# A threshold that two engines may take, and two accumulators in one tile

## The chip, the cores and the metric

The kernel runs on one core of one Trainium2 chip. The metric is the device time of one execution in microseconds (us). The engines are named as in the profile: PE (TensorE matmul), PEld (its weight loads), DVE (VectorE), ACT (ScalarE), POOL (GpSimd) and SP (the queue that issues most transfers).

## The reference

Eight batches, eight heads, 576 positions, head size 64. Attention keeps only the scores that lie within tau of their row's maximum; the result, seen as x of 512 channels, goes through a gated mixing layer:

```python
scores = scale * np.matmul(q, k.transpose(0, 1, 3, 2))
thresh = np.max(scores, axis=-1, keepdims=True) - tau
scores = np.where(scores >= thresh, scores, -1000000000.0)
attn = np.exp(scores - np.max(scores, axis=-1, keepdims=True))
attn = attn / (np.sum(attn, axis=-1, keepdims=True) + 1e-09)
attn_out = np.matmul(attn, v)
x = attn_out.transpose(0, 2, 1, 3).reshape(B, S, H * D)
gate_pre = sum(conv_w[k] * xp[:, k:k + S, :] for k in range(5))   # xp: x shifted in by 4 zeros
gate = 1.0 / (1.0 + np.exp(-gate_pre))
out = (gate * (x @ w_val)) @ w_out
```

## The kernel before, in words

**Tiles.** The work is cut into 32 jobs, one for each pair of heads of a batch. A job has nine score tiles of 128 rows by 576 keys: four for each head and one that holds the last 64 rows of both heads. There are 288 such tiles in all. For each tile PE makes the scores `s` in one of two PSUM rooms (`multiply`, L498), DVE finds the negated row maximum into column 0 of `nm` (`largest`, L502), and ACT makes the exponential `e` (`weigh`, L508). The threshold is one number for each row: the maximum less tau. It goes into column 1 of `nm`, and in the kernel before ACT computes it right behind the exponential (L510), as part of the same planned operation. DVE then masks the exponential where the score reaches the threshold, and sums the row (`keep`, L524); this frees the room of `s`. POOL adds a small constant to the sums (L541), DVE takes the reciprocal (L543), POOL or ACT divides (L554, L550), PE transposes (L604) into two `tp` rooms, and ACT copies the transposed tile to `T` (L615).

**Halves and accumulators.** When the tiles of half a job are there, PE multiplies `T` by `v` into an accumulator `acc` (`attend`, L643 and L650), and ACT copies it to `xT` (L658). A half is 320 or 256 columns. After the fourth job of a batch come the products with `w_val` and `w_out` (`products`, L742): 16 groups of 12 matmuls for each batch, each group into an accumulator. A group's result leaves through DVE (`g`, L769, for `w_val`) or ACT (`o`, L807, for `w_out`). So there are 64 accumulations of each of the three kinds. Each matmul of a product must follow the one before it. There are two accumulator rooms, `r_acc`, shared by all three kinds; in the kernel before they are two tiles of their own, [P, 512] each, one PSUM bank each.

**Order.** Nothing is issued in the order of the code. `op` describes an operation: the engine or engines that may do it, a due time, a cost and a time after which its result is there, what it must follow, which rooms it takes and which it gives back. `carry_out` then picks, again and again, the operation that can begin first (the earlier due time wins among equals), emits it on its engine, and so writes the instruction stream of every engine. An operation with more than one way (`other=`) goes to the engine where it can begin first. Before, only the division has two ways, POOL and ACT (`DIVIDE`). Each engine executes its own stream in that order. The waits between engines come from a layer below, which looks at which tiles an instruction reads and writes and adds semaphore waits.

Of the kernel before, what the change touches and what calls it, by code (L numbers as in the profile page):

```python
# [10 lines left out]
F32 = mybir.dt.float32  # L11
# [3 lines left out]
AF = mybir.ActivationFunctionType  # L15
# [2 lines left out]

P = 128
AHEAD = False  # L20
TH = "ACT"
DIVIDE = ("ACT",)
DUE = (8, 8, 8)
PACE_M = 0.17


@with_exitstack
def tile_thresholded_attention_gated_mix(
# [149 lines left out]
    r_s = Rooms(ps_s, 2, [P, 2, 512], F32, "s")  # L178
# [63 lines left out]
    class Words:  # L242


        def __init__(self, u, name, w, c, d0, before):
            due = u * 3.0 - 4
# [33 lines left out]
    def subtract(due, n, get, after, takes=(), gives=()):  # L280


        w = n // 2
        for cols in (slice(0, w), slice(w, n)):
            def run(cols=cols):
                dst, whole, high = get()
                nc.gpsimd.tensor_sub(dst[:, cols], whole[:, cols], high[:, cols].bitcast(F32))  # L287

            cost = w * 0.00237 + 0.04
            after = [op("POOL", due, cost, cost + 0.1, run, after, takes)]  # L290
            takes = ()
        after[0].gives = list(gives)
        return after[0]


    class Job:


        def __init__(self, i, b, g, at):
            self.i, self.b, self.g, self.at = i, b, g, at  # L300
            due = at - 9

            def fetch_v():
                self.v = r_v.take()
                nc.sync.dma_start(self.v, vs[b, g])

            self.got_v = op("SP", at - 3, 0.5, 3.6, fetch_v, takes=[r_v])
            if i == 0:
                self.load_at_once()
            else:  # L310
                self.prepare(due)

        def prepare(self, due):
# [24 lines left out]
            def low_q():  # L338
                if not hasattr(self, "ql"):
                    self.ql = r_ql.take()  # L340
                return self.ql, self.q_r, self.qh

            def scale_q():
                nc.gpsimd.tensor_scalar(self.q_r, self.q_r, sc, 0.0, op0=ALU.mult, op1=ALU.add)

# [4 lines left out]
            scaled = op("POOL", due, 0.75, 0.86, scale_q, [got_q])  # L350
            high = op("ACT", due + 1, 0.58, 0.76, high_q, [scaled], [r_qh])
            low = subtract(due + 2, S, low_q, [high], [r_ql], [(r_qr, lambda: self.q_r)])

            def place(which):
                def run():
# [91 lines left out]
    class Tile:  # L447
        def __init__(self, k, t, h, qc, grp):
            self.k, self.t, self.h, self.qc, self.grp = k, t, h, qc, grp
            i = h or 0  # L450
            both = h is None
            if both:
                after = [t.high_k, t.low_k, *t.blocks]
            elif t.i == 0:
                after = [t.first[h]]
            else:
                after = t.copied
            if tiles:
# [25 lines left out]

        def multiply(self):
            t, h, qc = self.t, self.h, self.qc
            s = self.s = r_s.take()
            for a in range(2):
                hs = slice(a * HS, (a + 1) * HS)
                if h is None:  # L490
# [15 lines left out]
        def weigh(self):  # L506
            self.e = r_e.take()
            nc.scalar.activation(self.e, self.s[:, :, :HS], AF.Exp, bias=self.nm[:, 0:1])  # L508
            if TH == "ACT":
                nc.scalar.activation(  # L510
                    self.nm[:, 1:2], self.nm[:, 0:1], AF.Identity, bias=less, scale=-1.0
                )

        def level(self):
            nc.vector.tensor_scalar(
# [14 lines left out]
    class Group:  # L530
# [5 lines left out]
        def turned(self, k):  # L536
# [4 lines left out]
            add = op("POOL", k - 4, 0.2, 0.33, lambda: nc.gpsimd.tensor_scalar(  # L541
                sums(), sums(), 1.0, 1e-9, op0=ALU.mult, op1=ALU.add), [self.kept])
            inv = op("DVE", k - 4.9, 0.08, 0.33, lambda: nc.vector.reciprocal(ri(0, n), sums()), [add])  # L543
            divided = []

            def divide(i, engine):
# [11 lines left out]
            others = {"DVEp": (0.44, 0.57), "ACT": (0.68, 0.83)}  # L558
            for i in range(n):
                divided.append(op(  # L560
                    "POOL", k - 4 + 0.1 * i, 0.74, 0.82, divide(i, "POOL"), [inv],
                    gives=[(r_sums, lambda: self.sums)] if i == n - 1 else [],
                    other=[(e, *others[e], divide(i, e)) for e in DIVIDE],
                ))
            if self.both:
                divided.append(op("POOL", k - 4, 0.21, 0.3, lambda: spread(
                    self.p[:, S : S + SL], self.p[:, S - SL : S]), divided))
            parts = [(0, NKC), (NKC, 1)] if self.both else [(0, 3), (3, 3), (6, 3)]
            out = []
            for c0, m in parts:  # L570
                last = c0 + m == (NKC + 1 if self.both else 2 * NKC + 1)
                half = self.half
                turn = op(
                    "PE", k - 3 + 0.1 * c0, 0.109 * m, 0.109 * (m - 1) + 0.35, self.turn(c0, m),
                    divided if last else divided[0 : 1 + c0 // 3 * (n - 1)], [r_tp],
                    [(r_pl if self.both else r_pp, lambda: self.p)] if last else [],
                )
# [2 lines left out]
                if not half.begun:  # L580
                    takes, half.begun = [r_T], True
                out.append(op(
                    "ACT", k - 3 + 0.1 * c0, cost, cost + 0.17, self.copy(c0, m), [turn, *half.room], takes,
                    [(r_tp, lambda c0=c0: self.tp[c0])],
                ))
                if takes:
# [44 lines left out]
    class Half:  # L631
# [4 lines left out]
        def attended(self, k):  # L636
# [18 lines left out]
            def evacuate():  # L655
                if j == 0:
                    t.xT = r_xT.take()
                nc.scalar.copy(t.xT[:, x0 : x0 + w], self.acc[:, :w])  # L658
# [5 lines left out]
            made = op("PE", k - 2, cost, cost + 0.2, attend, [t.got_v, *self.copies], [r_acc], gives)  # L664
            cost = 0.31 if j == 0 else 0.255
            after = [made] if j == 0 else [made, t.got_x]
            t.got_x = op("ACT", k - 4, cost, cost + 0.2, evacuate, after, [r_xT] if j == 0 else [],
                         [(r_acc, lambda: self.acc)])


    class Batch:
# [182 lines left out]
    for t in jobs:  # L854
# [3 lines left out]
        for j in range(2):  # L858
# [12 lines left out]
        convolve(t, batch, len(tiles))  # L871
        if t.g == NP - 1:
            last = products(batch, len(tiles) + 4.0, last)
    carry_out()


# [41 lines left out]
```

## Time and profile before

| | |
|---|---|
| time, median of 3 runs | 766.35 us (765.61 to 766.81) |
| the profiled execution | 766.39 us, its span 764.6 us |
| PE busy | 714.2 us (93%), 5216 matmul records |
| DVE busy | 617.5 us (81%) |
| ACT busy | 640.9 us (84%) |
| POOL busy | 544.1 us (71%) |
| granted TensorE clock, mean | 0.990 |
| chain that ended last | PE 71%, DVE 8%, ACT 7%, POOL 6%, DMA 4%, issue 3% |

A group of instructions is shown as line, engine, operation, output and inputs, shapes and count, then busy us and mean ns of one, then the idle time before them and what ended it. Matmuls are pipelined: the distance of two starts is what one costs the engine, and a record's own length is longer than that, with an end that is modelled.

### The profile page before, as it was taken

The numbers are of one execution on the slowest core, as the hardware profiler recorded it, in microseconds if no ns is written. First come the engines' busy times: TensorE is split into PE (matmuls) and PEld (weight loads), VectorE is DVE, ScalarE is ACT, GpSimd is POOL, SyncE is SP. The second block draws the span as 40 slices with busy tenths as digits, with TensorE's granted clock in tenths as the row PEclk, the third lists the DMA queues.
The fourth block names the chain that finished last, engine by engine and source line by source line (L and its number), as shares of the span: only waits on it lengthen the run. The fifth ranks groups of instructions, "written<-read, shape, count | busy, mean of one in ns | idle before, by whom it ended". The sixth has DMA issues, their size and how long they took to land.

```text
span 764.6 us, 15851 instructions
## 1 busy us (share of the span) xinstructions
PE 714.2 (93%) x5216; PEld 602.7 (79%) x5216; DVE 617.5 (81%) x1308; ACT 640.9 (84%) x1469; POOL 544.1 (71%) x885
## 2 busy tenths in 40 slices
PE   3687889979999999999999999999999999999997
PEld 3465557767788888888888888888888888888897
DVE  5878999989888878888888787888778988888630
ACT  5788987888889989989998898899889898988832
POOL 3677777778778867787678776688668876775431
PEclk9989999999999999999999999999999999999999
DMA  6746635344665556555555456455455455540001
GB/s 186 182 127 162 168 106 121 109 116 122 177 169 135 129 145 155 154 120 127 141 141 130 124 141 171 123 130 151 123 141 135 125 147 156 141 107 20 32 32 63
DMA packets 51890, 99.05 MB, mean 130 GB/s; under 512 B 9056, under 2 KB 9056, under 8 KB 51808
## 3 DMA queue, kind: packets, MB, share of 16 engines
q1 hardware_dynamic: 51488, 97.47, 49.0%
q8 instruction: 42, 0.69, 0.4%
q10 hardware_dynamic: 320, 0.56, 0.3%
q14 instruction: 40, 0.33, 0.1%
HBM read 35.74 MB, written 9.44 MB: 59 GB/s over the span
## 4 chain that ended last, share of the span: by engine, by line
PE 71%; DVE 8%; ACT 7%; POOL 6%; DMA 4%; issue 3%; SPq 1%; POOLq 0%; ACTq 0%
PE acc L742 20%; PE s L498 17%; PE acc L650 15%; PE tp L604 14%; PE acc L643 4%; DVE nm L502 3%; DMA q_r<-qT 2%; DVE pp L524 2%; ACT e L508 2%; ACT T L615 1%; DVE pre L700 1%; POOL pp L554 1%; POOL xl L287 1%; DMA KL<-kl 1%; POOL gl L287 1%
## 5 line engine op out<-in xcount | busy, mean ns | idle before, releaser
L502 DVE TENSOR_REDUCE nm<-s 128x1 f32<-128x576 f32 x288 | 215.8, 753 | 54.0 <-PE s L498 50.4
L508 ACT ACTIVATE e<-s,nm 128x576 f32<-128x576 f32 x288 | 215.5, 748 | 25.1 <-DVE nm L502 13.0
L524 DVE SCALAR_TENSOR_TENSOR pp<-s,nm,e 128x576 f32<-128x576 f32 x256 | 207.3, 813 | 35.1 <-ACT nm L510 31.7
L615 ACT COPY T<-tp 128x384 f32<-128x384 f32 x384 | 175.3, 487 | 27.6 <-PE tp L604 26.0
L604 PE MATMUL tp<-ident,pp 128*128 128x128 f32 x1152 | 182.3, 277 | 13.0 <-POOL pp L554 6.6
L498 PE MATMUL s<-KH,Q 128*128 128x288 f32 x512 | 162.1, 332 | 19.2 <-DVE Q L434 8.8
L554 POOL TENSOR_SCALAR pp<-pp,sums 128x576 f32<-128x576 f32 x174 | 142.5, 824 | 36.5 <-DVE sums L543 25.2
L604 PEld LDWEIGHTS tp<-ident,pp 128*128 128x128 f32 x1152 | 139.3, 142 | 23.2 <-POOL pp L554 10.1
L498 PE MATMUL s<-KL,Q 128*128 128x288 f32 x512 | 145.9, 299 | 0.7 <-DMA KL<-kl 0.7
L650 PE MATMUL acc<-T,v 128*64 128x256 f32 (+1 forms) x1024 | 138.3, 412 | 0.0
L498 PEld LDWEIGHTS s<-KH,Q 128*128 128x128 f32 x512 | 99.2, 194 | 43.3 <-DVE pp L524 13.8
L700 DVE SCALAR_TENSOR_TENSOR pre<-xT,cw,pre 128x576 f32<-128x576 f32 x128 | 119.2, 931 | 11.1 <-POOL pre L693 11.0
L650 PEld LDWEIGHTS acc<-T,v 128*64 128x64 f32 x1024 | 67.8, 136 | 62.9 <-issue 24.9
L498 PEld LDWEIGHTS s<-KL,Q 128*128 128x128 f32 x512 | 99.1, 194 | 0.9 <-DMA KL<-kl 0.9
L510 ACT ACTIVATE nm<-nm,less 128x1 f32<-128x1 f32 x288 | 85.0, 295 | 0.0
L742 PE MATMUL acc<-gl,woh 128*128 128x320 f32 (+1 forms) x256 | 78.1, 305 | 4.1 <-POOL gl L287 4.1
L742 PE MATMUL acc<-xl,wvh 128*128 128x320 f32 (+1 forms) x256 | 78.7, 307 | 2.6 <-POOL xl L287 2.5
L541 POOL TENSOR_SCALAR sums<-sums 128x2 f32<-128x2 f32 (+1 forms) x160 | 47.5, 297 | 45.5 <-DVE pp L524 33.2
L742 PE MATMUL acc<-gh,woh 128*128 128x320 f32 (+1 forms) x256 | 78.9, 308 | 0.7 <-ACT o L807 0.7
L742 PE MATMUL acc<-xh,wvl 128*128 128x320 f32 (+1 forms) x256 | 79.3, 310 | 0.0
L742 PE MATMUL acc<-xh,wvh 128*128 128x320 f32 (+1 forms) x256 | 78.4, 306 | 0.7 <-DVE g L769 0.5
L742 PE MATMUL acc<-gh,wol 128*128 128x320 f32 (+1 forms) x256 | 78.4, 306 | 0.0
(79 smaller groups left out, 1273.9 us busy)
## 6 DMA issues: line engine op xcount, KB each, us to landing
KH<-kh SPq DMA_DIRECT2D x124, 144.0 KB, 2.5
KL<-kl SPq DMA_DIRECT2D x124, 144.0 KB, 3.2
k_r<-kT SPq DMA_DIRECT2D x32, 320.0 KB, 3.7
v<-vs SPq DMA_DIRECT2D x32, 320.0 KB, 3.0
q_r<-qT SPq DMA_DIRECT2D x32, 288.0 KB, 2.9
outT<-o SPq DMA_DIRECT2D x32, 288.0 KB, 2.2
Q<-qh SPq DMA_DIRECT2D x62, 128.0 KB, 2.3
Q<-ql SPq DMA_DIRECT2D x62, 128.0 KB, 2.5
```

Source lines behind the costliest of these rows:

```text
L498: nc.tensor.matmul(s[:, a, :HS], w, m, start=i == 0, stop=i == len(terms) - 1)
L502: nc.vector.tensor_reduce(self.nm[:, 0:1], self.s[:, :, :HS], axis=AX.XY, op=ALU.max, negate=True)
L508: nc.scalar.activation(self.e, self.s[:, :, :HS], AF.Exp, bias=self.nm[:, 0:1])
L510: nc.scalar.activation(self.nm[:, 1:2], self.nm[:, 0:1], AF.Identity, bias=less, scale=-1.0)
L524: nc.vector.scalar_tensor_tensor(grp.p[:, i * S : (i + 1) * S].rearrange("p (a f) -> p a f", a=2), self.s[:, :, :HS], self.nm[:, 1:2], self.e,
L541: add = op("POOL", k - 4, 0.2, 0.33, lambda: nc.gpsimd.tensor_scalar(sums(), sums(), 1.0, 1e-9, op0=ALU.mult, op1=ALU.add), [self.kept])
L554: nc.gpsimd.tensor_scalar(v, v, ri(i), 0.0, op0=ALU.mult, op1=ALU.add)
L604: nc.tensor.transpose(tp[:, i * P : (i + 1) * P], self.p[:, k0 : k0 + P], ident)
L615: nc.scalar.copy(T[:, c0 : c0 + n, self.off : self.off + P], tp[:, 0 : n * P].rearrange("p (c q) -> p c q", q=P),)
L650: nc.tensor.matmul(acc[hs, :w], t.v[:, c0 : c0 + D], T[:, h * NKC + c, :], start=False, stop=c == NKC - 1, skip_group_check=True,)
L700: nc.vector.scalar_tensor_tensor(cv, t.xT[:, i : i + S], cw[:, g, i : i + 1], cv, op0=ALU.mult, op1=ALU.add)
L742: nc.tensor.matmul(taken[name, e, j][:, :w], wt[:, c, c0 : c0 + P], moving(c, i)[:, hs], start=n == 0, stop=n == NM - 1,)
```

## The change

The constant `TH` names two engines now, and the threshold becomes a planned operation of its own, apart from the exponential. It has two ways: on DVE (`level`) or on ACT (`level_act`), with a due time a little ahead of the exponential's. The exponential's planned cost falls from 0.83 to 0.64. Both must be there before `keep`.

The same diff turns several numbers of the planner into named constants of the same value (`AHEAD_D`, `AHEAD_T`, `AHEAD_A`, `AHEAD_J`, `LATE_X`, `LATE_M`, `CONVERT`), adds ways that are switched off (`SUB`, `QS`, `EXTRA`), and takes the two accumulators from one tile [P, 2, 512], of which each room is a half `accs[:, i, :]`.

```diff
-TH = "ACT"
+TH = ("DVE", "ACT")
 DIVIDE = ("ACT",)
+SUB = False
+EXTRA = 0
+QS = False
...
+    class Scores(Rooms):
+
+
+        def __init__(self, *args):
+            super().__init__(*args)
+            self.extra = None
+
+        def give(self, room, when):
+            if self.extra is not None and room is self.extra and retired:
+                self.extra = None
+                for i in range(2):
+                    r_acc.give(room[:, i, :], when)
+            else:
+                super().give(room, when)
+
+    retired = []
+    r_s = Scores(ps_s, 2, [P, 2, 512], F32, "s")
     r_tp = Rooms(ps_t, 2, [P, 512], F32, "tp")
-    r_acc = Rooms(ps_a, 2, [P, 512], F32, "acc")
+    r_acc = Rooms(ps_a, 1, [P, 2, 512], F32, "acc")
+    if EXTRA:
+        r_s.extra = r_acc.take()
+        r_s.give(r_s.extra, 0.0)
+    else:
+        accs = r_acc.take()
+        for i in range(2):
+            r_acc.give(accs[:, i, :], 0.0)
...
             if TH == "ACT":
                 after = [op("ACT", k - DUE[1], 0.83, 1.0, self.weigh, [largest], [r_e])]
             else:
+                ways = {"ACT": (0.19, 0.33, self.level_act), "DVE": (0.13, 0.2, self.level)}
+                first, *rest = TH
                 after = [
                     op("ACT", k - DUE[1], 0.64, 0.78, self.weigh, [largest], [r_e]),
-                    op("DVE", k - 9, 0.13, 0.13, self.level, [largest]),
+                    op(first, k - 8.5, *ways[first], [largest], other=[(w, *ways[w]) for w in rest]),
                 ]
...
+        def level_act(self):
+            nc.scalar.activation(
+                self.nm[:, 1:2], self.nm[:, 0:1], AF.Identity, bias=less, scale=-1.0
+            )
+
         def level(self):
             nc.vector.tensor_scalar(
                 self.nm[:, 1:2], self.nm[:, 0:1], -1.0, less, op0=ALU.mult, op1=ALU.add
...
             def attend():
-                acc = self.acc = r_acc.take()
+                acc = self.acc = rooms.take()
...
+            rooms = r_tp if EXTRA and t.b == 0 and k < EXTRA + 4 else r_acc
```

The planner's new choices give every engine another order of the same work. By the built streams, 124 of the 288 thresholds stand on DVE and 164 on ACT; 161 of those 164 stand directly ahead of an exponential. ACT has 106 divisions instead of 86, POOL 182 instead of 202. All other operations keep their engines and counts. Three places show what the prediction speaks of. In brackets is the engine whose semaphore an instruction waits for.

DVE at the first tiles of the run, before (TENSOR_REDUCE makes the maximum, the SCALAR_TENSOR_TENSOR on `pp` is the masking) and then now:

```order
L502 TENSOR_REDUCE nm_125<-s_101 128x1 [waits PE_49]
L502 TENSOR_REDUCE nm_126<-s_102 128x1 [waits PE_49]
L224 TENSOR_SCALAR cw_173<-cw_raw 128x20 [waits DMAHW0_49]
L524 SCALAR_TENSOR_TENSOR pp_131,sums_133<-s_101,nm_125,e_123 128x576 [waits Activation_49]
L524 SCALAR_TENSOR_TENSOR pp_131,sums_133<-s_102,nm_126,e_124 128x576 [waits Activation_49]
```

```order
L557 TENSOR_REDUCE nm_124<-s_101 128x1 [waits PE_49]
L575 TENSOR_SCALAR nm_124<-nm_124,less 128x1 [waits DVE_49]
L557 TENSOR_REDUCE nm_125<-s_102 128x1 [waits PE_49]
L584 SCALAR_TENSOR_TENSOR pp_130,sums_132<-s_101,nm_124,e_122 128x576 [waits DVE_49,Activation_49]
L584 SCALAR_TENSOR_TENSOR pp_130,sums_132<-s_102,nm_125,e_123 128x576 [waits Activation_49]
```

The first tile's threshold (L575) stands on DVE behind its maximum; the second's does not stand here.

ACT at the same tiles, before and now:

```order
L508 ACTIVATE e_123<-s_101,nm_125 128x576 [waits DVE_49]
L510 ACTIVATE nm_125<-nm_125,less 128x1
L336 CAST qh_111<-q_r_108 128x576 [waits Pool_49]
L508 ACTIVATE e_124<-s_102,nm_126 128x576 [waits DVE_49]
L510 ACTIVATE nm_126<-nm_126,less 128x1
```

```order
L563 ACTIVATE e_122<-s_101,nm_124 128x576 [waits DVE_49]
L373 CAST qh_110<-q_r_107 128x576 [waits Pool_49]
L570 ACTIVATE nm_125<-nm_125,less 128x1 [waits DVE_49]
L563 ACTIVATE e_123<-s_102,nm_125 128x576 [waits PE_49]
```

The second tile's threshold (L570) is on ACT, ahead of the exponential rather than behind it.

PE among the last products with `w_out`, at the start of a group of 256 columns, before and now (`gh`, `gl` are the two parts of `g`, `woh`, `wol` those of the weights):

```order
L742 MATMUL acc_106<-gh_158,woh 128x256 [waits Activation_49]
L742 MATMUL acc_106<-gl_162,woh 128x256
L742 MATMUL acc_106<-gh_158,wol 128x256
L742 MATMUL acc_106<-gh_159,woh 128x256
L742 MATMUL acc_106<-gl_163,woh 128x256
```

```order
L803 MATMUL acc_105<-gh_157,woh 128x256
L803 MATMUL acc_105<-gl_161,woh 128x256
L803 MATMUL acc_105<-gh_157,wol 128x256 [waits Activation_49]
L803 MATMUL acc_105<-gh_158,woh 128x256
L803 MATMUL acc_105<-gl_162,woh 128x256
```

Both rooms are the tile `acc_105` now, and the wait stands on the group's third matmul instead of its first. Before, that first wait was for the evacuation of the same room two groups earlier; now the wait on the third is for the evacuation of the other half, the group just before.

More of the change, by code (lines that the diff above doesn't have):

```diff
@@ L20 @@
 AHEAD = False
-TH = "ACT"
+TH = ("DVE", "ACT")
 DIVIDE = ("ACT",)
+SUB = False
+EXTRA = 0
+QS = False
 DUE = (8, 8, 8)
+AHEAD_D = 4
+AHEAD_T = 3
+AHEAD_A = 2
+AHEAD_J = 9
+LATE_X = 0
+LATE_M = 4.0
+CONVERT = (3.0, -4)
 PACE_M = 0.17
@@ L176, in carry_out @@
         assert not any(open_ops.values()), "some operations can never begin"
-    r_s = Rooms(ps_s, 2, [P, 2, 512], F32, "s")
-    r_tp = Rooms(ps_t, 2, [P, 512], F32, "tp")
-    r_acc = Rooms(ps_a, 2, [P, 512], F32, "acc")
+    class Scores(Rooms):
[11 more added lines that the diff above has]
+    r_s = Scores(ps_s, 2, [P, 2, 512], F32, "s")
+    r_tp = Rooms(ps_t, 2, [P, 512], F32, "tp")
+    r_acc = Rooms(ps_a, 1, [P, 2, 512], F32, "acc")
[6 more added lines that the diff above has]
+            r_acc.give(accs[:, i, :], 0.0)
     r_kr = Rooms(raw, 1, [P, SK], F32, "k_r")
@@ L245, in __init__ @@
         def __init__(self, u, name, w, c, d0, before):
-            due = u * 3.0 - 4
+            due = u * CONVERT[0] + CONVERT[1]
             hi, lo = (t[:, c, d0 : d0 + CW] for t in w_hl[name])
@@ L284, in subtract, with run @@
         for cols in (slice(0, w), slice(w, n)):
-            def run(cols=cols):
+            def run(engine, cols=cols):
                 dst, whole, high = get()
-                nc.gpsimd.tensor_sub(dst[:, cols], whole[:, cols], high[:, cols].bitcast(F32))
+                engine.tensor_sub(dst[:, cols], whole[:, cols], high[:, cols].bitcast(F32))
             cost = w * 0.00237 + 0.04
-            after = [op("POOL", due, cost, cost + 0.1, run, after, takes)]
+            fast = w * 0.00116 + 0.07
+            after = [op(
+                "POOL", due, cost, cost + 0.1, lambda run=run: run(nc.gpsimd), after, takes,
+                other=[("DVEp", fast, fast + 0.12, lambda run=run: run(nc.vector))] if SUB else [],
+            )]
             takes = ()
@@ L300, in __init__ @@
             self.i, self.b, self.g, self.at = i, b, g, at
-            due = at - 9
+            due = at - AHEAD_J
             def fetch_v():
@@ L341, in low_q, with high_scaled, low_scaled @@
                 return self.ql, self.q_r, self.qh
+            def high_scaled():
+                self.qh = r_qh.take()
+                nc.scalar.mul(self.qh, self.q_r, sc)
+            def low_scaled():
+                self.ql = r_ql.take()
+                nc.vector.scalar_tensor_tensor(
+                    self.ql, self.q_r, sc, self.qh.bitcast(F32), op0=ALU.mult, op1=ALU.subtract
+                )
             def scale_q():
@@ L349, in prepare @@
             self.low_k = subtract(due + 1, SK, low_k, [self.high_k], [r_kl], [(r_kr, lambda: self.k_r)])
-            scaled = op("POOL", due, 0.75, 0.86, scale_q, [got_q])
-            high = op("ACT", due + 1, 0.58, 0.76, high_q, [scaled], [r_qh])
-            low = subtract(due + 2, S, low_q, [high], [r_ql], [(r_qr, lambda: self.q_r)])
+            if QS:
+                high = op("ACT", due + 1, 0.6, 0.78, high_scaled, [got_q], [r_qh])
+                low = op("DVEp", due + 2, 0.74, 0.87, low_scaled, [high], [r_ql], [(r_qr, lambda: self.q_r)])
+            else:
+                scaled = op("POOL", due, 0.75, 0.86, scale_q, [got_q])
+                high = op("ACT", due + 1, 0.58, 0.76, high_q, [scaled], [r_qh])
+                low = subtract(due + 2, S, low_q, [high], [r_ql], [(r_qr, lambda: self.q_r)])
             def place(which):
@@ L487, in multiply @@
             s = self.s = r_s.take()
+            if self.k >= EXTRA:
+                retired.append(self.k)
             for a in range(2):
@@ L512, in weigh @@
                 )
+        def level_act(self):
+            nc.scalar.activation(
+                self.nm[:, 1:2], self.nm[:, 0:1], AF.Identity, bias=less, scale=-1.0
+            )
         def level(self):
@@ L540, in turned @@
             ri = lambda i, m=1: self.sums[:, 2 + i : 2 + i + m]
-            add = op("POOL", k - 4, 0.2, 0.33, lambda: nc.gpsimd.tensor_scalar(
+            add = op("POOL", k - AHEAD_D, 0.2, 0.33, lambda: nc.gpsimd.tensor_scalar(
                 sums(), sums(), 1.0, 1e-9, op0=ALU.mult, op1=ALU.add), [self.kept])
-            inv = op("DVE", k - 4.9, 0.08, 0.33, lambda: nc.vector.reciprocal(ri(0, n), sums()), [add])
+            inv = op("DVE", k - AHEAD_D - 0.9, 0.08, 0.33, lambda: nc.vector.reciprocal(ri(0, n), sums()), [add])
             divided = []
@@ L560, in turned @@
                 divided.append(op(
-                    "POOL", k - 4 + 0.1 * i, 0.74, 0.82, divide(i, "POOL"), [inv],
+                    "POOL", k - AHEAD_D + 0.1 * i, 0.74, 0.82, divide(i, "POOL"), [inv],
                     gives=[(r_sums, lambda: self.sums)] if i == n - 1 else [],
@@ L565, in turned @@
             if self.both:
-                divided.append(op("POOL", k - 4, 0.21, 0.3, lambda: spread(
+                divided.append(op("POOL", k - AHEAD_D, 0.21, 0.3, lambda: spread(
                     self.p[:, S : S + SL], self.p[:, S - SL : S]), divided))
@@ L573, in turned @@
                 turn = op(
-                    "PE", k - 3 + 0.1 * c0, 0.109 * m, 0.109 * (m - 1) + 0.35, self.turn(c0, m),
+                    "PE", k - AHEAD_T + 0.1 * c0, 0.109 * m, 0.109 * (m - 1) + 0.35, self.turn(c0, m),
                     divided if last else divided[0 : 1 + c0 // 3 * (n - 1)], [r_tp],
@@ L582, in turned @@
                 out.append(op(
-                    "ACT", k - 3 + 0.1 * c0, cost, cost + 0.17, self.copy(c0, m), [turn, *half.room], takes,
+                    "ACT", k - AHEAD_T + 0.1 * c0, cost, cost + 0.17, self.copy(c0, m), [turn, *half.room], takes,
                     [(r_tp, lambda c0=c0: self.tp[c0])],
@@ L663, in attended @@
                 gives.append((r_v, lambda: t.v))
-            made = op("PE", k - 2, cost, cost + 0.2, attend, [t.got_v, *self.copies], [r_acc], gives)
+            made = op("PE", k - AHEAD_A, cost, cost + 0.2, attend, [t.got_v, *self.copies], [rooms], gives)
             cost = 0.31 if j == 0 else 0.255
             after = [made] if j == 0 else [made, t.got_x]
-            t.got_x = op("ACT", k - 4, cost, cost + 0.2, evacuate, after, [r_xT] if j == 0 else [],
-                         [(r_acc, lambda: self.acc)])
+            t.got_x = op("ACT", k - AHEAD_A - 2, cost, cost + 0.2, evacuate, after, [r_xT] if j == 0 else [],
+                         [(rooms, lambda: self.acc)])
     class Batch:
@@ L870, in tile_thresholded_attention_gated_mix @@
             half.attended(len(tiles) - 1)
-        convolve(t, batch, len(tiles))
+        convolve(t, batch, len(tiles) + LATE_X)
         if t.g == NP - 1:
-            last = products(batch, len(tiles) + 4.0, last)
+            last = products(batch, len(tiles) + LATE_M, last)
     carry_out()
```

## The prediction

> **What bounds the kernel now.** I read the stages first, then TensorE's own waits in the middle of the run. The stage view gives, for each stretch, busy time and instruction count of each engine, the granted clock, the DMA share and GB/s:
>
> ```profile
> core 0: us, PE busy (x) PEld busy (x) DVE busy (x) ACT busy (x) POOL busy (x), PEclk, DMA share, GB/s
> 20.00:60.00 40.00, 30.09 (x182) 21.72 (x181) 32.43 (x77) 32.86 (x78) 28.72 (x50) 0.91 0.65 165
> 60.00:100.00 40.00, 32.97 (x215) 23.87 (x214) 37.09 (x82) 35.55 (x84) 30.35 (x52) 0.96 0.54 141
> 100.00:200.00 100.00, 86.76 (x620) 71.95 (x617) 91.84 (x196) 81.44 (x190) 74.58 (x120) 0.98 0.50 132
> 300.00:400.00 100.00, 99.98 (x755) 84.99 (x754) 82.54 (x175) 90.75 (x209) 74.30 (x118) 1.00 0.54 138
> 600.00:700.00 100.00, 100.00 (x763) 86.94 (x762) 85.71 (x181) 90.22 (x209) 72.75 (x116) 1.00 0.48 123
> ```
>
> From 200 us on PE has no free time, while DVE and ACT have 9 to 18%. A busy PE may hide waits under modelled ends, so I looked at what ended PE's idle time between 300 and 700 us, by group (after the second bar: idle us and its releasers):
>
> ```profile
> L604 PE MATMUL tp<-ident,pp 128*128 128x128 f32 x669 | 104.2, 273 | 0.6 <-ACT T L615 0.4 <-POOL pp L554 0.2
> L498 PE MATMUL s<-KH,Q 128*128 128x288 f32 x294 | 90.9, 325 | 0.9 <-DVE pp L524 0.8
> ```
>
> These two rows hold the only idle time of PE there: 1.5 us in 400, of which 0.8 us is a wait for a score buffer that the thresholding frees. So in the steady part TensorE sets the pace. Whatever makes a threshold come sooner has at most 1.5 us to win per 400; whatever stops PE adds itself to the end. Only in the first 100 us does PE wait for the chain through the threshold:
>
> ```profile
> PE tp L604 <- POOL pp L554: 6.5, 8, 1.8
> PE tp L604 <- ACT T L615: 4.3, 6, 1.2
> PE s L498 <- DVE pp L524: 3.1, 5, 2.0
> PE s L498 <- DVE pl L524: 1.3, 1, 1.3
> ```
>
> (waiter, releaser: us in total, times, longest), together 15.2 us.
>
> **The change, part one: the thresholds.** Of 288 one-column operations 124 go to DVE and 164 stay on ACT, nearly all now ahead of the exponential instead of behind it.
>
> ```profile
> L510 ACT ACTIVATE nm<-nm,less 128x1 f32<-128x1 f32 x288 | 85.0, 295 | 0.0
> L550 ACT ACTIVATE pp<-pp,sums 128x576 f32<-128x576 f32 x82 | 63.5, 776 | 5.6 <-DVE sums L543 5.2
> L543 DVE RECIPROCAL sums<-sums 128x2 f32<-128x2 f32 (+1 forms) x160 | 24.5, 156 | 12.4 <-POOL sums L541 11.6
> L87 DVE TENSOR_SCALAR less<-tau_sb 128x1 f32<-128x1 f32 x1 | 0.1, 144 | 0.0
> 304.11 0.75 ACT L508 ACTIVATE e<-s,nm 128x576 f32<-128x576 f32 x1
> 304.75 0.29 ACT L510 ACTIVATE nm<-nm,less 128x1 f32<-128x1 f32 x1
> 304.93 0.86 ACT L615 COPY T<-tp 128x384 f32<-128x384 f32 x2
> 305.12 0.81 DVE L524 SCALAR_TENSOR_TENSOR pp<-s,nm,e 128x576 f32<-128x576 f32 x1
> ```
>
> ACT starts the next operation 0.18 us after the threshold's start, so it loses 124 x 0.18 = 22 us of work. DVE gains 124 x 0.15 (the 144 and 156 ns rows) = 19 us. Twenty divisions also move from POOL to ACT, 20 x 0.78 = 16 us. On the path of one tile, the masking at 305.12 followed the threshold's end at 305.04; with the threshold elsewhere it can follow the exponential's end at 304.86, 0.18 us sooner. After 200 us this is hidden behind a full PE. In the first 100 us some 288 x 100/765 = 38 tiles pass, 43% of them with the threshold on DVE: at most 16 x 0.18 = 3 us, at least nothing. I take **-2**. If PE's cover were gone, the same count over the run would give 124 x 0.18 = 22 us; no row speaks for that.
>
> **Part two: the accumulators.** Before, the two accumulator rooms are two tiles; now they are two halves of one tile [P, 2, 512]. The planner sees two rooms either way. But in the built program the waits are set by tile. I followed each wait's count to the instruction that reaches it. Before, no accumulator matmul waits for the evacuation of the other room. Now 158 do, most in the middle of a product (the order shown ahead of this has one on the third matmul of the product), and 108 evacuations wait for a matmul into the other half which they do not read. PE executes in order, so everything behind such a matmul stands too: scores, transposes, the next product.
>
> The price comes from the end of the run, where products stand alone. The last matmul of a group, its evacuation, and a PE restart on another engine's release:
>
> ```profile
> 738.50 0.31 PE L742 MATMUL acc<-xl,wvh 128*128 128x320 f32 x1
> 738.65 0.31 PE L742 MATMUL acc<-xh,wvl 128*128 128x320 f32 x1
> 738.80 0.28 PE L742 MATMUL acc<-xh,wvh 128*128 128x256 f32 x1
> 738.91 0.28 PE L742 MATMUL acc<-xl,wvh 128*128 128x256 f32 x1
> 739.00 0.49 DVE L769 SCALAR_TENSOR_TENSOR g<-pre,acc 128x320 f32<-128x320 f32 x1 [0.77 <-PE acc L742]
> 739.03 0.28 PE L742 MATMUL acc<-xh,wvl 128*128 128x256 f32 x1
> 747.96 1.54 POOL L287 TENSOR_TENSOR gl<-g,gh 128x288 fp32r<-128x288 f32 x2 [1.60 <-ACT gh L785]
> 749.56 0.41 PE L742 MATMUL acc<-gl,woh 128*128 128x320 f32 x1 [1.21 <-POOL gl L287]
> 749.81 0.31 PE L742 MATMUL acc<-gh,wol 128*128 128x320 f32 x1
> ```
>
> From the start of the awaited matmul (738.65) to the start of its evacuation (739.00) are 0.35 us; from the release (747.96 + 1.54 = 749.50) to the restart 0.06. The evacuations last
>
> ```profile
> L769 DVE SCALAR_TENSOR_TENSOR g<-pre,acc 128x320 f32<-128x320 f32 x64 | 28.6, 447 | 8.7 <-PE acc L742 8.5
> L807 ACT ACTIVATE o<-acc 128x320 f32<-128x320 f32 x64 | 26.7, 418 | 11.6 <-PE acc L742 11.3
> L658 ACT COPY xT<-acc 128x320 f32<-128x320 f32 x64 | 25.3, 395 | 22.7 <-PE acc L650 22.0
> ```
>
> about 0.43 us. So matmul, evacuation, next matmul takes 0.35 + 0.43 + 0.06 = 0.84 us, where PE now spends one slot of 0.12 (738.80 to 738.91) to 0.15 (738.50 to 738.65), mean 0.13: 0.71 us lost. The restarted matmul also held its slot for 0.25 us (749.56 to 749.81) instead of 0.15: 0.10 more. Each wait with nothing to cover it costs **0.81 us**.
>
> How many are covered? I counted the PE instructions between the matmul that the evacuation waits for and the matmul that waits for the evacuation. For 46 of the 158 there are none: 46 x 0.81 = 37.3. Two have one: 2 x 0.68 = 1.4. For 21 there are three, mostly transposes or score matmuls, 0.39 us: 21 x 0.42 = 8.8. Six have four, 0.57 us: 6 x 0.24 = 1.4. Sixty-seven have five or more (at least 0.75 us of PE work): 0. For 16 the evacuation carries no PE wait of its own because an earlier instruction of its engine had it; between 0 and 0.81 each, I take 0.2: 3.2. Sum **+52**. The bounds: without the restart's 0.10, and with the 16 free, 46 x 0.71 + 2 x 0.58 + 21 x 0.32 + 6 x 0.14 = 41; with the 16 in full, 62.
>
> This supposes DVE or ACT free when the matmul is done. They are 82 to 91% busy in the stage rows, with operations of some 0.75 us: a wait of half of one in 80% of the 75 stopping cases is 75 x 0.8 x 0.375 = 22 us at most; nothing at least, since an evacuation stands in the order where its engine was planned free, and PE's stop lets it catch up. I take **+6**.
>
> The Trainium skill (Perfetto Trace Analysis, section Matmuls) says that independent matmul groups should rotate through different PSUM banks so that the evacuation of one overlaps the next group's matmuls. The matmuls at 738.80 to 739.03 run on under the evacuation and agree with it for before. The two halves still lie in different banks, so by that rule the sum would be 766.39 - 2 = 764; the built waits speak against it, and it stands as a rival below.
>
> **Sum.** The profiled execution took 766.39 us (span 764.6 and 1.8 around it), the median of the timed runs is 766.35, so nothing has to be converted. 766.39 - 2 + 52 + 6 = 822.4, forecast **822 us**, 1.07 times before. By the bounds of the terms: 766.4 - 3 + 41 + 0 = 804 to 766.4 - 0 + 62 + 22 = 850.
>
> **The rivals.** One row more is needed for the first, DVE's waits for score matmuls over the whole span:
>
> ```profile
> DVE nm L502 <- PE s L498: 50.4, 101, 1.9
> ```
>
> *Halves in different banks cost nothing* (chance 0.06). The mechanism: the evacuations run early enough, before PE reaches the waiting matmul, at all 158 places. What decides is whether PE lags behind ACT and DVE by more than 0.71 us at each of them; the row above speaks a little for it, as DVE does wait for a lagging PE. Then the thresholds alone count: 766.4 - 2 = 764, with 748 if all 22 us of ACT's relief came through. Against it: for 46 waits the evacuation itself needs the very matmul just before, and no lag helps there. Not slower than before in this case.
>
> *Only the end pays* (0.08). Behind the last score and transpose the product matmuls stand alone and nothing covers 14 waits: 14 x 0.81 = 11. In the middle half of the remaining 41 might be taken up in pauses between groups that the modelled ends hide: 766.4 + 11 + 20 - 3 = 794.
>
> *The stops spread* (0.06). The 108 evacuations that now wait for a matmul of the other half hold ACT and DVE, in order, with exponentials and reductions behind them. At up to 0.35 us each that is 38 us on engines with 9 to 18 us free per 100; if it all reached PE the time would be 822 + 38 = 860.
>
> *The clock sinks* (0.05). In the stage rows the clock goes with PE's pauses: 0.91 with 25% idle, 0.96 with 18%, 0.98 with 13%, 1.00 with none. Here 58 of 822 us idle are 7%, which lies between 0.98 and 1.00. At 0.98 throughout, 822 x 0.02 = 16 us: 838. The Trainium skill (TensorE: Matmul & The Clock Gate, section A second HAM failure mode: psum-queue depth-cycling) describes a kernel whose short idles between matmul groups made the clock swing between half and full; the stage rows show nothing near half, so I keep the small price.
>
> **How the numbers follow.** The forecast has 0.75, with its own range 804 to 850; the clock's 838 lies inside it. The 794 of the second rival sits near its foot. To leave no more than 2 in 10 outside I go from 792 to 850; outside lie the first rival, the third and the edges. What counts as no change here is within 0.2%, 1.5 us. Faster by more than that: most of the first rival, 0.04; within: 0.02; slower: 0.94.
>
> **What would show it.** Right: in the last 30 us the third matmul of nearly each product is idle 0.6 to 0.7 us with the releaser o or g; PE's idle between 300 and 700 us rises from 1.5 to some 25 us, on accumulator rows, with the evacuations as releasers; PE busy falls to about 93%; ACT's threshold rows are 164, DVE's 124 at about 150 ns. Wrong: accumulator rows without idle time, or a PE that waits mainly for scores' buffers or transposes. The forecast fails if the waits land where PE stood anyway, or if ACT and DVE, not PE, become the engines without free time.

## The result, and the profile after

The changed kernel takes 834.91 us (median of 4 runs, 834.07 to 837.4) against 766.58 us for the kernel before, run beside it: 1.0899 times as long, 95% interval 1.0874 to 1.0924. The forecast was 822 us, 1.07 times; the direction and the place were right, the time was 13 us longer than that.

The stages of the changed kernel, in the columns of the prediction's first fence (from the profiled execution, span 832.3 us):

```profile
core 0: us, PE busy (x) PEld busy (x) DVE busy (x) ACT busy (x) POOL busy (x), PEclk, DMA share, GB/s
20.00:60.00 40.00, 32.95 (x189) 24.56 (x188) 32.33 (x80) 31.26 (x70) 28.31 (x52) 0.87 0.63 152
60.00:100.00 40.00, 30.77 (x201) 22.99 (x200) 35.61 (x88) 34.80 (x76) 29.77 (x53) 0.96 0.58 154
100.00:200.00 100.00, 81.85 (x527) 64.42 (x526) 91.18 (x215) 80.30 (x170) 71.59 (x115) 0.91 0.47 125
300.00:400.00 100.00, 96.20 (x714) 81.97 (x713) 80.69 (x182) 82.92 (x179) 67.85 (x111) 1.00 0.49 127
600.00:700.00 100.00, 95.26 (x703) 79.90 (x697) 80.12 (x180) 82.17 (x175) 67.97 (x110) 1.00 0.46 123
```

Between 300 and 400 us PE starts 714 matmuls instead of 755, at a granted clock of 1.00 in both, and all other engines have more free time than before. Where PE stands is in the waits. First PE's weight loads on accumulator rows, then PE's matmuls there (us in total, times, longest):

```profile
PEld acc L803 <- DVE g L830: 27.5, 42, 0.9
PEld acc L803 <- ACT o L868: 26.5, 42, 0.8
PE acc L803 <- DVE g L830: 17.5, 41, 0.7
PE acc L803 <- ACT o L868: 16.6, 38, 0.6
PEld acc L803 <- ACT xT L718: 5.2, 7, 1.3
```

The product matmuls (L803) wait for the three kinds of evacuation: 91 stops of the weight loads, 59.2 us in all (27.5 + 26.5 + 5.2). In the trace before, there was one such stop for `o` and one for `g`, 1.7 us of weight loads' idle time together:

```profile
PEld acc L742 <- ACT o L807: 1.0, 1, 1.0
PEld acc L742 <- DVE g L769: 0.7, 1, 0.7
```

And the last products of the changed kernel, as the timeline has them:

```profile
818.72 0.28 PE L803 MATMUL acc<-gl,woh 128*128 128x256 f32 x1
818.84 0.28 PE L803 MATMUL acc<-gh,wol 128*128 128x256 f32 x1
818.95 0.31 PE L803 MATMUL acc<-gh,woh 128*128 128x320 f32 x1
819.10 0.31 PE L803 MATMUL acc<-gl,woh 128*128 128x320 f32 x1
819.51 0.38 ACT L868 ACTIVATE o<-acc 128x256 f32<-128x256 f32 x1 [1.89 <-PE acc L803]
819.94 0.19 PEld L803 LDWEIGHTS acc<-gh,wol 128*128 128x128 f32 x1 [0.80 <-ACT o L868]
819.94 0.41 PE L803 MATMUL acc<-gh,wol 128*128 128x320 f32 x1 [0.53 <-ACT o L868]
820.19 0.31 PE L803 MATMUL acc<-gh,woh 128*128 128x320 f32 x1
```

Here is the whole mechanism in eight rows. The evacuated group of 256 columns ended with the matmul at 818.84. Its evacuation starts at 819.51 only, after two matmuls of the next group that write the other half. The third matmul of that group stands until the evacuation is done: 819.10 to 819.94 is 0.84 us, the forecast's sum, where the slot is 0.15. The parts differ a little and offset each other: 0.41 us to the evacuation, 0.38 for it and 0.05 back, where the forecast had 0.35, 0.43 and 0.06. The third matmul then holds its own slot for 0.25 us (819.94 to 820.19). Lost are 0.79 us. The row of the weight load shows 0.80 us of idle time, the row of the matmul only 0.53, since a matmul's modelled end covers the rest. So the weight loads' idle time is the better measure of these stops. The same shows over 400 us, first before, then now:

```profile
300.00:700.00 400.00, 398.57 (x3009) 342.18 (x3008) 335.08 (x704) 357.88 (x822) 298.71 (x480) 1.00 0.52 134
```

```profile
300.00:700.00 400.00, 382.64 (x2803) 321.00 (x2801) 321.69 (x717) 333.06 (x710) 269.45 (x442) 1.00 0.49 128
```

PE starts 6.8% fewer matmuls; its busy time fell by 4.0%, the weight loads' by 6.2%. The Trainium skill (Trainium Kernel Development and Optimization, section Performance Expectations) says that matmul busy time is a bad metric for how close a kernel is to roofline, because matmuls are pipelined, and the weight loads' busy share a good one. These rows agree: the weight loads' 6.2% lies nearer to the 6.8% of the matmuls started.

### The profile page after: what moved, and what is told of

Its sections match the earlier page's. It is cut to its first block, busy times and chain, and to the rows that moved or that the text cites. A ratio compares the mean times of both kernels' runs of the same rounds, so it can differ in the third digit from the quotient of the medians.

```text
span 832.3 us, 15842 instructions
## 1 busy us (share of the span) xinstructions
PE 743.4 (89%) x5216; PEld 611.5 (73%) x5216; DVE 634.5 (76%) x1432; ACT 642.8 (77%) x1365; POOL 523.9 (63%) x865
## 4 chain that ended last, share of the span: by engine, by line
PE 76%; DVE 11%; ACT 7%; issue 3%; POOL 1%; DMA 1%; POOLq 0%; SPq 0%; DVEq 0%; ACTq 0%
PE acc L803 25%; PE s L553 19%; PE acc L710 15%; PE tp L664 14%; PE acc L703 4%; DVE pp L584 2%; DVE nm L557 2%; DVE g L830 2%; ACT o L868 2%; ACT e L563 2%; DVE pre L761 1%; ACT T L675 1%; ACT xT L718 1%; DMA o<-w_val 0%; DMA pp<-kT 0%
## 5 line engine op out<-in xcount | busy, mean ns | idle before, releaser
L584 DVE SCALAR_TENSOR_TENSOR pp<-s,nm,e 128x576 f32<-128x576 f32 x256 | 206.1, 812 | 29.6 <-ACT e L563 26.5
L563 ACT ACTIVATE e<-s,nm 128x576 f32<-128x576 f32 x288 | 209.8, 739 | 10.9 <-DVE sums L603 6.9
L553 PE MATMUL s<-KH,Q 128*128 128x288 f32 x512 | 164.2, 336 | 31.6 <-DVE pp L584 17.7
L614 POOL TENSOR_SCALAR pp<-pp,sums 128x576 f32<-128x576 f32 x155 | 127.7, 829 | 57.6 <-DVE sums L603 39.0
L664 PEld LDWEIGHTS tp<-ident,pp 128*128 128x128 f32 x1152 | 141.8, 143 | 11.8 <-ACT T L675 4.6
L761 DVE SCALAR_TENSOR_TENSOR pre<-xT,cw,pre 128x576 f32<-128x576 f32 x128 | 115.7, 904 | 19.7 <-POOL pre L754 19.5
L803 PE MATMUL acc<-gh,wol 128*128 128x320 f32 (+1 forms) x256 | 80.8, 316 | 11.8 <-ACT o L868 9.4
L601 POOL TENSOR_SCALAR sums<-sums 128x2 f32<-128x2 f32 (+1 forms) x160 | 40.7, 254 | 77.6 <-DVE pp L584 67.4
L803 PE MATMUL acc<-xh,wvl 128*128 128x320 f32 (+1 forms) x256 | 79.8, 312 | 8.4 <-DVE g L830 7.9
L803 PE MATMUL acc<-xl,wvh 128*128 128x320 f32 (+1 forms) x256 | 80.1, 313 | 7.5 <-DVE g L830 4.5
L803 PE MATMUL acc<-gl,woh 128*128 128x320 f32 (+1 forms) x256 | 79.8, 312 | 5.8 <-ACT o L868 2.5
L610 ACT ACTIVATE pp<-pp,sums 128x576 f32<-128x576 f32 x101 | 77.9, 780 | 7.3 <-DVE sums L603 7.2
L803 PE MATMUL acc<-gh,woh 128*128 128x320 f32 (+1 forms) x256 | 79.5, 310 | 3.3 <-ACT o L868 2.2
L803 PE MATMUL acc<-xh,wvh 128*128 128x320 f32 (+1 forms) x256 | 79.3, 310 | 3.5 <-DVE g L830 2.7
```

Of the source, the lines that this page charges most:

```text
L553: nc.tensor.matmul(s[:, a, :HS], w, m, start=i == 0, stop=i == len(terms) - 1)
L584: nc.vector.scalar_tensor_tensor(grp.p[:, i * S : (i + 1) * S].rearrange("p (a f) -> p a f", a=2), self.s[:, :, :HS], self.nm[:, 1:2], self.e,
L601: add = op("POOL", k - AHEAD_D, 0.2, 0.33, lambda: nc.gpsimd.tensor_scalar(sums(), sums(), 1.0, 1e-9, op0=ALU.mult, op1=ALU.add), [self.kept])
L610: nc.scalar.mul(v, v, ri(i))
L614: nc.gpsimd.tensor_scalar(v, v, ri(i), 0.0, op0=ALU.mult, op1=ALU.add)
L664: nc.tensor.transpose(tp[:, i * P : (i + 1) * P], self.p[:, k0 : k0 + P], ident)
```

## The experiments

**Two tiles again.** Everything of the change stays, the plan too; only the accumulators become two tiles.

```diff
-    r_acc = Rooms(ps_a, 1, [P, 2, 512], F32, "acc")
-    if EXTRA:
-        r_s.extra = r_acc.take()
-        r_s.give(r_s.extra, 0.0)
-    else:
-        accs = r_acc.take()
-        for i in range(2):
-            r_acc.give(accs[:, i, :], 0.0)
+    r_acc = Rooms(ps_a, 2, [P, 512], F32, "acc")
```

> The changed kernel with the accumulators as two tiles again; the planner's order, and so every engine's stream, stays that of the changed kernel, and no accumulator matmul waits for the other room any more. Theory (the waits between the halves of one tile are the whole cost): 760 to 768 us, idle time of PE on accumulator rows back under 10 us. Rival A (the waits are the 56 us of the forecast, and the other 12 us come from the new order of the work, in the start above all): 774 to 782 us. Rival B (the thresholds' new places are the cost): 820 us or more.

It took 771.87 us, 1.0057 times the kernel before (1.004 to 1.0074). So 63 of the 68 us are the shared tile. The time lies 4 us above the theory's range and 2 below rival A's, so 5 us need another cause; rival B falls. PE's product matmuls are idle for 2.8 us in all, under the expected 10; the group with the most idle time over the whole span is now

```profile
L796 PE MATMUL acc<-gl,woh 128*128 128x320 f32 (+1 forms) x256 | 78.9, 308 | 1.2 <-POOL gl L313 1.2
```

**The kernel before, in one tile.** The converse: no threshold is moved, the order is that of before.

```diff
-    r_acc = Rooms(ps_a, 2, [P, 512], F32, "acc")
+    r_acc = Rooms(ps_a, 1, [P, 2, 512], F32, "acc")
+    accs = r_acc.take()
+    for i in range(2):
+        r_acc.give(accs[:, i, :], 0.0)
```

> The kernel before, with thresholds on ACT behind the exponential and its own order, but the two accumulators as halves of one tile. Built, 157 accumulator matmuls wait for the other half's evacuation, 61 of them with no PE instruction between. Theory: 61 x 0.81 = 49, the partly covered ones 8, the 15 unknown ones 3, busy engines 6: 766 + 66 = 832 us (815 to 850). Rival B (the thresholds are the cost): 764 to 770 us.

837.17 us, 1.0906 times (1.0881 to 1.0932), within 5 us of the 832 worked out from the built waits. Its stops on weight loads:

```profile
PEld acc L745 <- DVE g L772: 36.1, 50, 0.9
PEld acc L745 <- ACT o L810: 26.5, 43, 0.8
PEld acc L745 <- ACT xT L661: 4.0, 5, 1.7
```

98 stops, 66.6 us, for a loss of 70 us. The shared tile alone, without any moved threshold, makes the kernel as slow as the whole change does.

**All thresholds on one engine, two tiles.**

```diff
-TH = ("DVE", "ACT")
+TH = ("DVE",)
```

> Two accumulator tiles, and all 288 thresholds on DVE. DVE gains 288 x 0.21 = 60 us of work, ACT loses 288 x 0.18 = 52. Theory (PE sets the pace): 760 to 770 us, within 1% of the run with both ways. Rival (DVE becomes the bound: 617 + 60 = 678 us busy of some 765, 89%): 775 us or more.

775.01 us, 1.0104 times (1.0059 to 1.015): above the theory's 760 to 770, at the foot of the rival's range, and 3 us (0.4%) above the run with both ways, inside the 1% that the theory also named. By its time alone the run does not refute the rival. The trace speaks against its mechanism: from 300 to 700 us PE is busy 99.6 to 100 of each 100 us and DVE 87 to 88, so PE still sets the pace there. In the profiled run the granted clock was 0.92 between 200 and 300 us, where PE starts 644 matmuls; with both ways it was 1.00, with 760. Whether the 3 us are more than that is not shown.

```diff
-TH = ("DVE", "ACT")
+TH = ("ACT",)
```

> Two accumulator tiles, and all 288 thresholds on ACT as an operation of its own, planned ahead of the exponential instead of behind it. Theory (PE sets the pace): 763 to 770 us, like the kernel before. If the two ways are worth what ACT is relieved of (22 us of work), this run should be several us slower than the run with both ways; if PE's cover holds, within 4 us of it.

765.44 us, 0.9987 times (0.9958 to 1.0015): no difference from the kernel before, and 6 us faster than with both ways. Relieving ACT bought nothing. In this pair it cost, by an amount that lies within the scatter between plans found below.

**The evacuation done twice.** To see whether the length of an evacuation is what PE waits for, each evacuation of the `w_out` products is written twice by ACT, in the changed kernel and in its two-tile form.

```diff
                         nc.scalar.mul(o[f][:, hs], taken["wo", f, j][:, 0 : hs.stop - hs.start], 0.5)
+                        nc.scalar.mul(o[f][:, hs], taken["wo", f, j][:, 0 : hs.stop - hs.start], 0.5)
```

> The changed kernel, with each of the 64 evacuations of the products with w_out done twice in a row on ACT (the same result written again; the plan does not know of it). Theory (PE stands until the other half's evacuation is done): some 40 of the stops are of this kind and each gets longer by one more evacuation, 0.25 to 0.4 us: 835 + 10 to 16 = 845 to 851 us. Rival (the stops have another cause, and evacuations are only named beside them): 835 to 838 us.

861.56 us, 1.1242 times (1.1211 to 1.1272), 27 us more than with single evacuations, where 10 to 16 were expected.

```profile
PEld acc L803 <- ACT o L869: 48.8, 53, 1.2
```

The 42 stops of 0.63 us on average (26.5 / 42) became 53 of 0.92 (48.8 / 53). On average each is 0.29 us longer, inside the expected 0.25 to 0.4; not expected were 11 more places at which the longer evacuation is no longer covered. These stops grew by 22.3 of the 27 us. The time misses the ranges of both theory and rival; that the stops for `o` are what grew speaks for the theory.

> The same doubled evacuation with two accumulator tiles. Theory (with two tiles an evacuation runs beside the next group, and ACT has free time): within 3 us of the run with two tiles and single evacuations. Rival (the doubling costs through ACT's own time, not through the wait): as much longer as the doubling makes the one-tile kernel, 10 us or more.

785.71 us, 1.0258 times (1.0233 to 1.0283), 14 us more than the two-tile run. That expectation failed: 64 further operations cost 14 / 64 = 0.22 us each although ACT has free time in every stage. So the doubling alone says less of the shared tile than was meant: it costs 27 us with one tile and 14 with two, and only the difference, 13 us, needs the shared tile. PE's waits between 300 and 600 us show one way in which the 14 us arise, first with two tiles and single evacuations, then doubled:

```profile
PEld tp L657 <- ACT T L668: 1.1, 2, 0.6
```

```profile
PEld tp L657 <- ACT T L668: 7.0, 16, 0.8
```

The extra operation stands on ACT ahead of a copy that frees a transpose buffer (`T` from `tp`), and PE, in order, waits for that buffer. Over the whole run this wait grows from 4.9 to 12.4 us, about half of the 14; where the rest arises is not shown. The product matmuls have no stop for `o`. So with two tiles a late ACT costs through the order of its queue, and with one tile mostly through the evacuation itself; the two are different waits. But the sentence that ACT's free time hides what is put on it does not hold here for work that the plan does not know of.

**Where the 5 us come from.** The two-tile run starts fewer matmuls than the kernel before in the first 200 us and more after. Before, and then with two tiles:

```profile
0.00:200.00 200.00, 158.07 (x1040) 124.74 (x1041) 172.16 (x379) 161.24 (x370) 141.80 (x243) 0.97 0.55 145
200.00:700.00 500.00, 496.38 (x3735) 424.88 (x3734) 418.57 (x879) 447.61 (x1028) 379.58 (x612) 1.00 0.53 135
```

```profile
0.00:200.00 200.00, 151.65 (x962) 116.12 (x964) 170.92 (x408) 159.85 (x338) 139.91 (x242) 0.95 0.55 143
200.00:700.00 500.00, 499.28 (x3786) 431.07 (x3783) 427.06 (x960) 441.24 (x949) 360.53 (x588) 1.00 0.53 136
```

It is 78 matmuls behind at 200 us and catches up 51 of them by 700. Two readings were open: thresholds on DVE hurt at the start, where DVE also converts the weights; or two plans of the same work simply differ. Five runs, all with two tiles, were made to part them.

```diff
-                first, *rest = TH
+                first, *rest = ("ACT",) if k < 80 else TH
```

> Two accumulator tiles; the thresholds of the first 80 tiles (some 200 us) on ACT ahead of the exponential, both ways only from tile 80 on (84 of 288 on DVE in all). Up to tile 80 the order is that of the run with all thresholds on ACT. Theory S (the 5 us that the two ways cost with two tiles arise in the first 200 us, where DVE also converts the weights and is 90% busy): 761 to 767 us, no slower than the run with all thresholds on ACT (765). Rival P (the 5 us are scatter between plans, of which the thresholds' place is only one cause): anywhere in 762 to 774 us. Rival L (the cost is in the steady part): 770 us or more.

766.77 us, 0.9996 times (0.9978 to 1.0014).

```diff
-                first, *rest = TH
+                first, *rest = TH if k < 80 else ("ACT",)
```

> The reverse: two ways for the first 80 tiles, then ACT alone (38 thresholds on DVE). The first 80 tiles stand as in the run with both ways all along. Theory S: 770 to 775 us. Rival L: 763 to 767 us.

774.24 us, 1.0093 times (1.007 to 1.0116). So far theory S: the cost goes with the first 80 tiles.

```diff
-                ways = {"ACT": (0.19, 0.33, self.level_act), "DVE": (0.13, 0.2, self.level)}
+                ways = {"ACT": (0.19, 0.33, self.level_act), "DVE": (0.21, 0.28, self.level)}
```

> Two accumulator tiles and both ways, with the planner told 0.21 for a threshold on DVE, as the profile has it (213 ns), instead of 0.13. 134 thresholds go to DVE. If the planner's wrong price is what costs the 5 us: 764 to 768 us. If not, it stays within 3 us of the run with the wrong price (772).

768.38 us, 1.0012 times (0.9997 to 1.0027): 3.5 us below the run with the wrong price, just outside both ranges, so it decides nothing.

```diff
-                ways = {"ACT": (0.19, 0.33, self.level_act), "DVE": (0.13, 0.2, self.level)}
+                ways = {"ACT": (0.2, 0.34, self.level_act), "DVE": (0.13, 0.2, self.level)}
```

> Two accumulator tiles and both ways, with the threshold's planned price on ACT 0.20 instead of 0.19: nothing that matters to the chip, but the plan comes out another (127 on DVE instead of 124, another order from the second job on). It measures how far two plans of the same work lie apart. Theory S, in which the first stage costs: 769 to 775 us. Rival P (scatter between plans): 5 us or more from the run with 0.19.

763.66 us, 0.9958 times (0.994 to 0.9975), 8 us below its neighbour, although 127 thresholds are on DVE instead of 124 and both ways are open at the start. Theory S as stated falls with this run: what the first 200 us take is a matter of the plan. In that stage PE's waits for the masking to free a score buffer are, with 0.19 and then with 0.20:

```profile
PE s L546 <- DVE pp L577: 21.2, 16, 2.7
```

```profile
PE s L546 <- DVE pp L577: 8.1, 12, 1.6
```

> Two accumulator tiles and both ways, the threshold's planned price on ACT 0.18 instead of 0.19 (120 thresholds on DVE). Rival P (plans of the same work scatter): between 762 and 775 us, without order by the price. Theory S (the two ways cost about 5 us in the first stage): 769 to 775 us.

769.86 us, 1.0029 times (1.0015 to 1.0043), inside both ranges. Four plans that all let a threshold go either way take 763.7, 768.4, 769.9 and 771.9 us, without order by the price. Their mean, 768.4, is within 2 us of the kernel before. A part of this scatter goes with the granted clock: of the runs with 0.20, those with a mean clock of 0.977 or 0.978 took 765.8 to 766.8 us and those with 0.991 took 761.9 to 762.0. But at nearly the same clock the plans still differ: 762.4 to 765.9 us with 0.20 at 0.984, and 770.2 to 770.7 with 0.19 at 0.986 or 0.987. The place of the thresholds is worth less than the scatter between plans, some 8 us from the best to the worst; whether it is worth anything stays open.

**The shared tile under another plan.**

> One accumulator tile with the plan of 0.20, whose two-tile form took 763.7 us. Built, 156 matmuls wait for the other half, 49 with no PE instruction between, 14 with three, 8 with four. By the forecast's prices: 49 x 0.81 + 1 x 0.68 + 14 x 0.42 + 8 x 0.24 + 18 x 0.2 = 52, and 6 for busy engines: 763.7 + 58 = 822 us (815 to 830). If the shared tile costs the same 63 us as in the first pair of runs: 827.

The edit is that of the 0.20 run, with the changed kernel's one tile. 830.6 us, 1.0813 times (1.0787 to 1.0839): 9 us above the 822 that the forecast's prices give and just outside their range, 4 above the 827 by the first pair. The three pairs differ in the accumulators' tile alone; as built, every engine has the same instructions in the same order in both kernels of a pair, and only the waits differ:

| plan | two tiles, us | one tile, us | difference | waits with no PE instruction between | forecast price |
|---|---|---|---|---|---|
| of the kernel before | 766.95 | 837.17 | 70 | 61 | 66 |
| of the change | 771.87 | 834.91 | 63 | 46 | 58 |
| with 0.20 | 763.66 | 830.60 | 67 | 49 | 58 |

(The one-tile figures of the second and third row were measured at other times than their partners; the kernel before had medians of 766.6 to 767.4 us beside them.) The price by counting waits is 4 to 9 us too low each time.

## Why the prediction was right, and where it was short

**PE sets the pace from 200 us on, so a stop of PE adds to the end.** Right. The 59.2 us that the weight loads stood for evacuations make up nearly all of the 63 us that the shared tile costs.

**What one bare stop costs: 0.81 us.** Right to 0.02 at the place shown (0.79): 0.84 us from matmul to matmul, though its three parts offset each other, and 0.25 for the restart's slot. Over the run a bare stop is 0.76 us of idle weight loads on average.

**How many stops, and how long: two mis-sized terms that offset each other.** Each wait of the built program can be found in the trace as one weight load. Sorted by the forecast's classes, their idle time (where it is longer than 150 ns) is:

| PE instructions between | waits | forecast, us | stopped | measured, us |
|---|---|---|---|---|
| none | 46 | 37.3 | 46 | 34.9 |
| one | 2 | 1.4 | 2 | 1.2 |
| three | 21 | 8.8 | 21 | 9.7 |
| four | 6 | 1.4 | 3 | 0.9 |
| five or more | 67 | 0 | 2 | 1.0 |
| the evacuation has no PE wait of its own | 16 | 3.2 | 16 | 10.7 |
| all | 158 | 52 | 90 | 58.3 |

(The 91st stop is one for an evacuation of the matmul's own room.) The count of what is covered was right: of the 67 waits taken as free only 2 stopped. The mis-sized term is the last class: each of the 16 stopped, for 0.67 us on average, where the forecast took 0.2. The other five classes measure 47.7 us against 48.9, so the +6 for busy engines is not to be seen there. So 52 + 6 = 58 meets the measured 58.3 in part by luck. The other two one-tile kernels show the same: 0.76 us for a bare stop, and 0.86 and 0.71 us for those of the last class that stopped.

The 13 us by which the forecast fell short are therefore elsewhere: some 7 in the thresholds' term below (-2 against +5), and some 5 in the shared tile (58 against 63). In each of the three pairs 4 to 7 us of the tile's cost stand in none of these stops; where they arise is open. The 108 evacuations named in the prediction are also not quite right: as built, 101 wait for a matmul into the other half, and 7 of these, which wait for another reader of that half as well, were counted twice.

**The thresholds: -2 us.** The wrong way: with two tiles the changed plan is 5 us slower than before, not 2 faster. The step that failed is that the forecast treated the order as the same but for the moved operations; the runs on prices show that another order of the same work is worth up to 8 us. The granted clock is lower with this plan too, 0.980 in the median of its runs against 0.991 before; by that ratio it would be worth up to 8 us, an estimate. Whether the plan's start lowers the clock or the clock takes the time, no run parts. That DVE pays 0.15 us for a threshold was low as well:

```profile
L575 DVE TENSOR_SCALAR nm<-nm,less 128x1 f32<-128x1 f32 x124 | 26.2, 213 | 1.5
L570 ACT ACTIVATE nm<-nm,less 128x1 f32<-128x1 f32 x164 | 49.0, 299 | 12.6 <-DVE nm L557 11.3
```

213 ns against the 144 and 156 ns rows. The counts, 124 and 164, are as built. Why the operation is longer was not tried: it reads what the reduction just ahead may have written, and it takes `less` as a second operand.

**Hidden behind a full PE.** For moved thresholds no run contradicts this argument by more than the scatter, but it does not hold in its strong form: 64 unplanned operations on ACT cost 14 us with two tiles.

**The rivals.** That halves in different banks cost nothing is refuted by three pairs. So, for this kernel, is the rule of the Trainium skill (Perfetto Trace Analysis, section Matmuls) that was weighed there, as far as it is read to mean that different banks are enough: the halves are in different banks, and still 90 of the 158 waits for the other half's evacuation stopped PE. What set the waits is the tile. That only the end pays (794) falls with the stops between 300 and 700 us. Stops that spread to 860 were not seen: the waits of `o` and `g` for product matmuls did grow by 35 us (11.3 + 8.5 us before, 29.1 + 25.4 now), near that rival's 38, but the time came out at 835. The clock did sink, from 0.990 to 0.981 on average, but at the start, where the stage rows have 0.87 and 0.91; the profiled two-tile run without the stops has a mean of 0.986 and 0.95 over the first 200 us. In the median of its runs the changed plan has 0.980 with one tile and with two, and the kernel before in one tile, with 98 stops, has 0.989 or more in each. So the lower clock does not come from the stops. Nor does it follow PE's idle share as the prediction read it: the new rows have 0.87 with 18% idle and 0.96 with 23%. From 200 us on it is 1.00 with PE 4 to 7% idle. The signs that were named came in part: the third matmul of a late product stands with `o` as releaser, as said, but for 0.5 to 0.6 us; PE's busy share between 300 and 700 us is 95 to 96% instead of 93, and its matmul idle time on product rows between 300 and 700 us is 16.6 us (the sum of 3.1, 4.0, 1.1, 4.2, 3.5 and 0.7 in the groups below) instead of 25, because the modelled ends hide a part of a stop (0.27 of 0.80 us in the one shown). The weight loads of the same groups are idle for 28.2 us there.

```profile
L803 PE MATMUL acc<-gh,wol 128*128 128x256 f32 (+1 forms) x151 | 47.3, 313 | 3.1 <-ACT o L868 2.6 <-ACT xT L718 0.4 <-DVE g L830 0.2
L803 PE MATMUL acc<-gl,woh 128*128 128x320 f32 (+1 forms) x150 | 47.1, 314 | 4.0 <-ACT o L868 2.5 <-DVE g L830 1.0 <-ACT xT L718 0.5
L803 PE MATMUL acc<-gh,woh 128*128 128x320 f32 (+1 forms) x150 | 46.7, 311 | 1.1 <-ACT o L868 1.0
L803 PE MATMUL acc<-xl,wvh 128*128 128x320 f32 (+1 forms) x129 | 40.9, 317 | 4.2 <-DVE g L830 3.3 <-ACT o L868 0.9
L803 PE MATMUL acc<-xh,wvl 128*128 128x320 f32 (+1 forms) x129 | 40.1, 311 | 3.5 <-DVE g L830 3.5
L803 PE MATMUL acc<-xh,wvh 128*128 128x320 f32 (+1 forms) x130 | 39.9, 307 | 0.7 <-DVE g L830 0.5 <-ACT o L868 0.2
```

## What to carry to other kernels

Read what a change does to tiles as well as to operations: two buffers that become halves of one tile may be tied together by waits that no line of the kernel asks for, and where the engine that stands is the one that sets the pace, each such wait that nothing covers costs its whole round (here about 0.8 us; of 158 waits 90 stopped PE, for 0.65 us on average). Follow the counts of the built waits for the engine that bounds, and price them from a place in the trace where the same round already stands bare. Where a planner sets the order, compare a change with several plans of the same work before it is credited or blamed for a per cent: here a planned price moved by 0.01 was worth 8 us, and the fastest version that ran (763.7 us, 0.4% ahead of the kernel before) is such a plan with two tiles.

## What the runs showed of the hardware that was not expected

A threshold on one column takes DVE 213 ns in 124 cases, against 144 to 156 ns for other one- and two-column operations. And ACT's free time is not free: with ACT 88 to 91 of 100 us busy in the stages from 200 to 700 us of the doubled two-tile run, 64 more operations of 411 ns, unknown to the plan, lengthened the run by 0.22 us each; about half of that shows in PE's waits for transpose buffers that ACT frees later.
